# Rotary attention and a routed feed-forward on one core: logits of the last two head pairs in four tiles, the second group's gather placed behind them, and the order of the feed-forward's first blocks

## The chip, the cores and the metric

The kernel runs on one core of a Trainium2 chip. The metric is the device time in microseconds of one execution. Below, PE is the matrix engine (PEld its weight loads), DVE the vector engine, ACT the scalar engine, POOL the GpSimd engine and SP the sync engine, which here only starts DMAs.

## What is computed

```python
q_rot, k_rot = rotate(q), rotate(k)                 # 8 batches, 8 heads, 576 rows, 64 columns
scores = scale * q_rot @ k_rot.T
attn = exp(scores - max(scores)) ; attn /= sum(attn)
x = (attn @ v) as rows                              # 4608 rows of 512
h_dense = maximum(x @ w1_dense, 0) ; y_dense = h_dense @ w2_dense
expert_idx = argmax(x @ w_gate)                     # one of 8 experts for each row
gate_w = softmax(x @ w_gate)[expert_idx]
h = maximum(x[mask] @ w1[e], 0)                     # for each expert e, its rows
out = y_dense + gate_w * (h @ w2[e])
```

## The kernel before, in words

**Attention.** The loop of `attention` (L716) goes over 32 pairs of heads (`NP`), four to a batch, and one more turn for the last pair's output. Each turn `i` has nine steps `t`. In step `t` three things are put into the engines' queues by hand: the row maxima of pair `i + 2` (`s1_block`, while there is such a pair), one strip of logits of pair `i` (`s2_strip`: PE writes 128 x 512 into a tile of the tag `s2`, ACT takes the exponent into `pm`, L402), and a part of the product with the values for pair `i - 1` (`av_part`, L424). The tag `s2` has two buffers of one bank. Behind the nine steps come the tails of the strips (`s2_tails`, L409). `av_scale` divides by the sums on DVE, and `x_store` writes a batch's rows `xn` to the DRAM tensor `xd` (L451, L452, on SP's queue).

**PSUM.** The pool `attn_ps` has the tags `s1` (two buffers of two banks), `s2` (two of one bank) and `av` (one of two banks). From pair 29 on the value products use `s1`, and `av` is used by the sums of the routing (`attn_sums`) in turn 30.

**Routing.** Rows are sorted by expert into tiles of 128 rows, 4 tiles to a group. The first part (batches 0 to 5, 20 tiles, 5 groups) is planned while the last pairs of attention run. Its result `num` gives `take_i` (which rows a tile gathers), `put_i`, `gp` and `woff`. The second part (batches 6 and 7) is planned during the feed-forward, one piece of `plan` behind each of the first 12 tiles.

**Gather.** `gather` (L841) is an indirect DMA on POOL's queue that brings a tile's 128 rows from `xd` to `xg`; `turn` (L847) is a transposing DMA on SP's queue from `xg` to `xs`. `fetch` is both. `draw(g, u0)` (L853) does two tiles of group `g`, with their row numbers converted on DVE just before (`rows_of`, L829). In the kernel before, `draw` is put at turns and steps (30, 2), (30, 6), (31, 2), (31, 6) and twice at (31, 7): three groups, 12 tiles, all before the end of attention.

**Feed-forward.** `run_groups` (L940) goes over the groups and their tiles. For a tile, `expert_in` (L888) is one block of four 512-column matmuls on PE, then the gate and the rectifier on ACT into `hn` (L896); `expert_turn` transposes `hn` into `he` by a DMA on SP's queue (L901); `out_tile` (L904) is two blocks on PE (L908 with the dense half, L910 with the expert's), a copy on DVE (L912) and an indirect DMA that scatters the rows (L913, POOL's queue). The dense first half of a group is four blocks (`dense_in`, L884), each with a rectifier on ACT (L886). Each block needs all four tiles' `xs`, since it has the group's 512 columns. Before the loop the first group's four dense blocks stand at once; then each tile has its expert block, one dense block of the next group, and, once more than three tiles are open (`advance(3)`), an `out_tile`. Gathers of later groups go one or two to a tile (L965 to L974), ahead of the tile's expert block.

Of the kernel before, what the change touches and what calls it, by code (L numbers as in the profile page):

```python
# [13 lines left out]
bf16 = mybir.dt.bfloat16  # L14
# [7 lines left out]
P = 128  # L22
# [3 lines left out]
def kernel(  # L26
# [370 lines left out]
    def s2_strip(i, s):  # L397
        if s == 0:
            state["pm", i] = ap.tile([P, 9, S], fp16, tag="pm", bufs=2, name="pm")
        ps = pp.tile([P, 512], f32, tag="s2", bufs=2, name="s2")  # L400
        s2_mm(i, ps, s, False)
        nc.scalar.activation(state["pm", i][:, ORDER.index(s), 0:MAIN], ps, AF.Exp, scale=float(scale))  # L402

    def s2_tails(i, part):
# [154 lines left out]
    def plan_steps(k, wp, psum, st):  # L559
# [68 lines left out]
        def f():  # L628
            ts = slice(t0, t0 + NK)
            p5 = wp.tile([P, NPT, NK], f32, tag="p5", name="p5", **tl)  # L630
            nc.vector.tensor_copy(p5, ps["pt"])
            num = wp.tile([P, NK], f32, tag="num", name="num", **tl)
            nc.vector.tensor_tensor(num, p5[:, 0], p5[:, 1], AL.add)

            if k == 0:
                nums.append(num)
                rows_of(0, 2)
                rest = slice(3 * GT, NK)
                nc.vector.tensor_scalar(take_i[:, rest], num[:, rest], scalar1=-1.0, scalar2=0.0, op0=AL.add, op1=AL.max)
# [23 lines left out]
    def attention():  # L663
# [52 lines left out]
        for i in range(NP + 1):  # L716
            for t in range(9):
                if i + 2 < NP:
                    s1_block(i + 2, t)
                if i < NP:  # L720
                    s2_strip(i, t)
                if 1 <= i <= NP and t >= 1:
                    for k in range(*AVS[i % HP == 1][t]):
                        av_part(i - 1, k)
                    if t == 8:
                        av_scale(i - 1)
                if i == 0 and t in (3, 5):
# [12 lines left out]
                if t == 2 and i + LA < NP:  # L740
                    stage_transpose(i + LA)
                if t == 2:
                    for f, *x in loads.pop(i, ()):
                        f(*x)
                if (i, t) in WS:
                    n = WS.index((i, t))
                    load_w(*((w1d, moe_w1_dense), (w2d, moe_w2_dense))[n] if n < 2 else (w1e[:, n - 2], moe_w1[n - 2]))
                if t == 5:

                    if i % HP == 0 and i // HP + 1 < B:  # L750
                        stage_v(i // HP + 1)
                    if i % HP == 3 and HP < i < NP - HP or i == NP - 3:
                        x_store(i // HP - 1)
                    if i == NP - RA:
                        early_cm.__exit__(None, None, None)
                        open_late()
                        wa = late["wa"]
                        pl, mm, fin = plan_steps(0, wa, attn_sums, got0)
                        w2 = [lambda e=e: load_w(late["w2e"][:, e], moe_w2[e]) for e in range(E)]
                        steps[27, 6] = rk[0:1] + [route_parts]  # L760
                        steps[27, 5] = w2[0:2]
                        steps[27, 7] = w2[2:5]
                        steps[28, 0] = rk[1:2] + w2[5:6] + pl[0:1]
                        steps[28, 2] = gt[3:4]
                        steps[28, 3] = rk[2:3] + w2[6:8] + pl[1:2]
                        steps[28, 6] = rk[3:4]
                        steps[29, 0] = pl[2:3]
                        steps[30, 5] = pl[3:4]
                        steps[29, 3] = pl[4:6]
                        steps[29, 8] = rk[4:5]  # L770
                        steps[30, 0] = rk[5:6]
                        steps[30, 2] = mm + [fin, lambda: draw(0, 0)]
                        for n, at in enumerate(((30, 6), (31, 2), (31, 6))):
                            steps[at] = [lambda n=n: draw((n + 1) // 2, 2 * (n + 1) % GT)]
                        steps[31, 7] = [lambda: draw(2, 0), lambda: draw(2, 2)]
                if (i, t) == (NP - 2, 4):
                    logit_sum(B - 2)
                for st in steps.pop((i, t), ()):
                    st()
            if i < NP:  # L780
                s2_tails(i, 0)
            if i < NP:
                s2_tails(i, 1)
            if i in (0, 1) or i < NP and i % HP == 0:
                u0, u1 = (2 * i, 2 * i + 2) if i < 2 else (0, HP)
                for u in range(u0, u1, 2):
                    v_gate(u)
                v_part(i // HP, 0, u0, u1)
                steps.setdefault((i + 1, 0), []).append(lambda b=i // HP, u0=u0, u1=u1: v_part(b, 1, u0, u1))
        assert not steps and not v_steps and not loads  # L790
        logit_sum(B - 1)
        x_store(B - 1)
# [30 lines left out]
    got = []  # L823

    nums = []

    def rows_of(t0, n):
        ts = slice(t0, t0 + n)
        nc.vector.tensor_scalar(take_i[:, ts], nums[0][:, ts], scalar1=-1.0, scalar2=0.0, op0=AL.add, op1=AL.max)  # L829

    def room(g, pool, tag, bufs):
        m = sizes[g] if bufs == 1 else GT
        xg = pool.tile([P, m, DG], bf16, tag=f"xg{tag}", bufs=min(bufs, 2), name="xg")
        xs = pool.tile([P, m, DT, P], bf16, tag=f"xs{tag}", bufs=bufs, name="xs")
        got.append((xg, xs))

    def gather(g, u):
# [15 lines left out]
    def draw(g, u0):  # L853
        if u0 == 0:
            room(g, late["first"], g, 1)
        if (g, u0) != (0, 0):
            rows_of(g * GT + u0, 2)
        for u in range(u0, u0 + 2):
            fetch(g, u)

# [27 lines left out]
    def expert_in(t, xs, u):  # L888
# [3 lines left out]
        for dt in range(DT):  # L892
            nc.tensor.matmul(ps, lhsT=xs[:, u, dt, :], rhs=w[:, 0, dt, :], start=(dt == 0), stop=(dt == DT - 1))  # L893

        hn = fp.tile([P, F], bf16, tag="hn", bufs=3, name="hn")
        nc.scalar.activation(hn, ps, AF.Relu, scale=gp[:, t:t + 1])  # L896
        return hn, e

# [41 lines left out]
    def run_groups(gs, plan):  # L940
# [9 lines left out]
                w = todo.pop(0)  # L950
                out_tile(w["t"], w["hd"], w["u"], w["he"], w["e"])

        ahead = [(g, u) for g in gs if g >= len(got) for u in range(sizes[g])]
        known = len(plan)
        turns = []
        for st in dense_steps(gs[0]):
            st()
        for g in gs:
            n = sizes[g]
            dense = dense_steps(g + 1) if g + 1 in gs else []  # L960
            for u in range(n):
                t = sum(sizes[:g]) + u
                while turns:
                    turn(*turns.pop(0))
                for w in range(2):  # L965
                    if not ahead or ahead[0][0] > g + 3 or t < known and ahead[0][0] >= G1:
                        break
                    h, x = ahead[0]
                    if w and sum(sizes[:h]) + x > t + 12:
                        break  # L970
                    if x == 0:
# [56 lines left out]
```

## Time and profile before

| | us |
|---|---|
| median of 3 runs | 471.67 (471.66 to 476.84) |
| the profiled execution's own time | 471.43 |
| its span in the profile | 469.7 |
| PE busy | 405.4 |
| POOL busy | 342.4 |
| DVE busy | 320.4 |
| ACT busy | 295.0 |

The profiled execution's own time is 1.7 us over its span; what is read from the profile is set against this execution. The profile's views name a wait by what ended it: "issue" is time for which the profile shows no cause, "remote" and "another core or an unknown queue" are signals whose sender it could not name. Times in a timeline are counted from the span's start. Attention's last matmul ends near 328.4 us, and the feed-forward takes the rest.

### The profile page before, as it was taken

The numbers are of one execution on the slowest core, as the hardware profiler recorded it, in microseconds if no ns is written. First come the engines' busy times: TensorE is split into PE (matmuls) and PEld (weight loads), VectorE is DVE, ScalarE is ACT, GpSimd is POOL, SyncE is SP. The second block draws the span as 40 slices with busy tenths as digits, with TensorE's granted clock in tenths as the row PEclk, the third lists the DMA queues.
The fourth block names the chain that finished last, engine by engine and source line by source line (L and its number), as shares of the span: only waits on it lengthen the run. The fifth ranks groups of instructions, "written<-read, shape, count | busy, mean of one in ns | idle before, by whom it ended". The sixth has DMA issues, their size and how long they took to land.

```text
span 469.7 us, 11058 instructions
## 1 busy us (share of the span) xinstructions
PE 405.4 (86%) x4093; PEld 251.7 (54%) x4108; DVE 320.4 (68%) x583; ACT 295.0 (63%) x566; POOL 342.4 (73%) x279
## 2 busy tenths in 40 slices
PE   1788898899999998998998978736999998999992
PEld 1346566666666666666665656524444543444440
DVE  7886799899899999999998899911367311121221
ACT  6587887887887887897897767624633232333320
POOL 1899999989999799899999769571353465662332
PEclk9998999999999999999999989966999999999998
DMA  6866649987858867988969999673467469885352
GB/s 185 225 162 157 157 111 240 164 194 210 182 171 207 201 164 223 172 169 234 153 169 219 155 189 211 134 183 87 130 174 164 124 169 202 212 184 154 102 136 91
DMA packets 134251, 80.65 MB, mean 172 GB/s; under 512 B 93461, under 2 KB 127765, under 8 KB 134197
## 3 DMA queue, kind: packets, MB, share of 16 engines
q1 hardware_dynamic: 119684, 55.93, 50.6%
q0 software_dynamic: 14240, 23.73, 23.2%
q8 instruction: 35, 0.57, 0.5%
q10 hardware_dynamic: 272, 0.26, 0.2%
q14 instruction: 20, 0.16, 0.1%
HBM read 52.05 MB, written 14.42 MB: 142 GB/s over the span
## 4 chain that ended last, share of the span: by engine, by line
PE 64%; DVE 11%; ACT 9%; DMA 8%; issue 3%; another core or an unknown queue 2%; SPq 1%; POOLq 0%; POOL 0%; ACTq 0%; DVEq 0%
PE s L369 10%; PE av L424 9%; PE s L392 9%; PE py L910 7%; PE pd L884 7%; PE py L908 7%; PE pe L893 7%; DVE negm L371 5%; ACT pm L402 5%; DMA qT<-mT 3%; DMA kx<-qT 2%; PE vps L281 2%; PE s L365 2%; PE s L389 2%
## 5 line engine op out<-in xcount | busy, mean ns | idle before, releaser
L371 DVE TENSOR_REDUCE negm<-s 128x1 f32<-128x576 f32 x288 | 205.2, 750 | 20.1 <-PE s L369 18.5
L402 ACT ACTIVATE pm<-s 128x512 f16<-128x512 f32 x288 | 166.0, 598 | 54.7 <-PE s L392 39.3
L392 PE MATMUL s<-qT,kx 128*128 128x512 bf16 (+1 forms) x510 | 111.2, 290 | 13.0 <-ACT pm L402 8.2
L424 PEld LDWEIGHTS <-pm 128*128 128x128 f16 x1600 | 88.9, 99 | 60.1 <-issue 28.2
L369 PE MATMUL s<-kx,qT 126*128 126x288 bf16 x512 | 108.6, 295 | 6.0 <-DVE negm L371 4.2
L424 PE MATMUL av<-v,pm 128*128 128x82 f16 x1600 | 102.5, 203 | 1.0 <-DVE v L300 0.5
L314 POOL TENSOR_TENSOR ra<-qk,cosx 128x1152 bf16<-128x1152 f32 x30 | 78.9, 2629 | 19.4 <-DVE nat L317 10.7
L912 DVE COPY y<-py 128x512 f32<-128x512 f32 x37 | 25.2, 690 | 82.8 <-PE py L910 56.9
L913 POOL DMA_INDIRECT out_dram<-y,put_i x37 | 38.2, 1033 | 59.4 <-DVE y L912 42.7
L317 POOL TENSOR_TENSOR nat<-ra,rb 128x1152 bf16<-128x1152 bf16 x30 | 70.9, 2364 | 2.4
L896 ACT ACTIVATE hn<-pe,gp 128x512 bf16<-128x512 f32 x37 | 25.4, 687 | 66.1 <-PE pe L893 31.7
L841 POOL DMA_INDIRECT xg<-xd,take_i x37 | 35.9, 969 | 30.4 <-DMA xd<-xn 14.8
L369 PEld LDWEIGHTS <-qT 126*128 126x128 bf16 x512 | 40.5, 100 | 20.4 <-issue 12.3
L392 PEld LDWEIGHTS <-kx 128*128 128x128 bf16 x512 | 35.7, 97 | 12.2 <-issue 4.3
L315 POOL TENSOR_TENSOR rb<-qk,sinx 128x576 bf16<-128x576 f32 x30 | 42.1, 1405 | 0.0
L316 POOL TENSOR_TENSOR rb<-qk,sinx 128x576 bf16<-128x576 f32 x30 | 42.1, 1403 | 0.0
L893 PE MATMUL pe<-w1e,xs 128*128 x145 | 37.6, 379 | 1.8 <-ACT hn L896 0.8
L884 PE MATMUL pd<-xs,w1d 128*128 128x512 bf16 (+1 forms) x160 | 38.0, 363 | 0.4 <-ACT hd L886 0.3
L910 PE MATMUL py<-w2e,he 128*128 x145 | 37.5, 379 | 0.2
L908 PE MATMUL py<-w2d,hd 128*128 128x512 bf16 x141 | 37.1, 379 | 0.3
L886 ACT ACTIVATE hd<-pd 128x512 bf16<-128x512 f32 (+1 forms) x40 | 22.6, 564 | 15.1 <-PE pd L884 7.2
L389 PE MATMUL s<-qT,kx 128*64 128x512 bf16 x64 | 18.5, 289 | 14.5 <-issue 6.3
(173 smaller groups left out, 427.9 us busy)
## 6 DMA issues: line engine op xcount, KB each, us to landing
vf<-in_v_dram SPq DMA_DIRECT2D x8, 1024.0 KB
qk<-in_q_dram SPq DMA_DIRECT2D x15, 512.0 KB
qk<-in_k_dram SPq DMA_DIRECT2D x15, 512.0 KB
kx<-qT SPq DMA_DIRECT2D x30, 144.0 KB
xd<-xn SPq DMA_DIRECT2D x8, 512.0 KB
w1e<-in_moe_w_dram POOLq DMA_DIRECT2D x8, 512.0 KB
w2e<-in_moe_w_dram POOLq DMA_DIRECT2D x8, 512.0 KB
vf<-in_v_dram SPq DMA_DIRECT2D x16, 64.0 KB
```

Of the source, the lines that this page charges most:

```text
L314: eng.tensor_tensor(a, x, cx, AL.mult)
L315: eng.tensor_tensor(s[:, :, :, 0:half], x[:, :, :, half:D], sx[:, :, :, 0:half], AL.mult)
L317: eng.tensor_tensor(nat.rearrange("p c w d -> p w c d"), a, s, AL.add)
L369: nc.tensor.matmul(ps[:, c, 0:CH], lhsT=qT[:, t * P:(t + 1) * P], rhs=kT[:, k0 + c * CH:k0 + (c + 1) * CH], start=True, stop=True)
L371: nc.vector.tensor_reduce(state["negm", i][:, t:t + 1], ps[:, :, 0:CH], axis=AX.XY, op=AL.max, negate=True)
L392: nc.tensor.matmul(out_ap, lhsT=kT[:, s * P:(s + 1) * P], rhs=qT[:, qa if s < 4 else qb], start=True, stop=True)
L402: nc.scalar.activation(state["pm", i][:, ORDER.index(s), 0:MAIN], ps, AF.Exp, scale=float(scale))
L424: nc.tensor.matmul(state["av"][:, h, x * VC:(x + 1) * VC], lhsT=state["pm", i][:, 4 * h + n if n < 4 else 8, q0:q0 + P], rhs=v16s[b % VB][ ...
L884: nc.tensor.matmul(ps[:, 0:n], lhsT=w1d[:, dt, ft * P:(ft + 1) * P], rhs=xs[:, 0:n, dt, :], start=(dt == 0), stop=(dt == DT - 1))
L893: nc.tensor.matmul(ps, lhsT=xs[:, u, dt, :], rhs=w[:, 0, dt, :], start=(dt == 0), stop=(dt == DT - 1))
L908: nc.tensor.matmul(py, lhsT=hd[:, ft, u], rhs=w2d[:, ft, :], start=(ft == 0), stop=False)
L910: nc.tensor.matmul(py, lhsT=he[:, ft], rhs=w[:, 0, ft, :], start=False, stop=(ft == FT - 1))
```

## The change

- `s2_strip`: for the last two pairs (30 and 31) the strips 2 and 3, and 6 and 7, are computed two at a time into one two-bank tile of the tag `av`; the exponents are taken one strip at a time as before.
- The row numbers of groups 1 and 2 are put into a float tile `tk` by one DVE instruction when the plan is ready. `draw(1, 0)` and `draw(1, 2)` stand behind the whole of turn 31; an ACT copy that converts group 1's numbers into `take_i` stands ahead of them, in ACT's queue behind the last exponent. Nothing of group 2 is gathered in attention.
- Group 2 is gathered in the feed-forward, one tile behind each of the first four expert blocks, each with a small ACT copy for its row numbers. The rooms of groups 2 and 3 are made at the beginning. From the fifth tile on two tiles are gathered to a tile, until the first part's 20 are done.
- The feed-forward begins with the first tile's expert block. The first group's dense blocks come 0, 1, 1 and 2 behind its four tiles; those of groups 1 and 2 come two to a tile in group 1. In group 0 no `out_tile` is done (`advance(GT)`). A tile's gathers come behind its expert block, not ahead. `hn` has four buffers in place of three, and `room` makes `xs` before `xg`.

```diff
-        ps = pp.tile([P, 512], f32, tag="s2", bufs=2, name="s2")
-        s2_mm(i, ps, s, False)
+        if i < NP - 2 or s not in (2, 3, 6, 7):
+            ps = pp.tile([P, 512], f32, tag="s2", bufs=2, name="s2")
+            s2_mm(i, ps, s, False)
+        else:
+            if s % 2 == 0:
+                state["s2"] = pp.tile([P, 2, 512], f32, tag="av", bufs=1, name="s2w")
+                for x in range(2):
+                    s2_mm(i, state["s2"][:, x], s + x, False)
+            ps = state["s2"][:, s % 2]
...
+                nc.vector.tensor_scalar(tk, num[:, GT:3 * GT], scalar1=-1.0, scalar2=0.0, op0=AL.add, op1=AL.max)
...
-                        for n, at in enumerate(((30, 6), (31, 2), (31, 6))):
-                            steps[at] = [lambda n=n: draw((n + 1) // 2, 2 * (n + 1) % GT)]
-                        steps[31, 7] = [lambda: draw(2, 0), lambda: draw(2, 2)]
+                        steps[30, 6] = [lambda: draw(0, 2)]
...
+            if i == NP - 1:
+                draw(1, 0)
+                draw(1, 2)
...
+        xs = pool.tile([P, m, DT, P], bf16, tag=f"xs{tag}", bufs=bufs, name="xs")
         xg = pool.tile([P, m, DG], bf16, tag=f"xg{tag}", bufs=min(bufs, 2), name="xg")
-        xs = pool.tile([P, m, DT, P], bf16, tag=f"xs{tag}", bufs=bufs, name="xs")
...
-        if (g, u0) != (0, 0):
-            rows_of(g * GT + u0, 2)
+        if u0 == 0 and g:
+            nc.scalar.copy(take_i[:, g * GT:(g + 1) * GT], tk[:, (g - 1) * GT:g * GT])
+        if (g, u0) == (0, 2):
+            rows_of(u0, 2)
...
-        ahead = [(g, u) for g in gs if g >= len(got) for u in range(sizes[g])]
+        begin = gs[0] == 0
+        ahead = [(g, u) for g in gs if g >= 2 for u in range(sizes[g])] if begin else []
+        if begin:
+            room(2, late["first"], 2, 1)
+            room(3, fp, "", 4)
...
-        for st in dense_steps(gs[0]):
-            st()
+        dense = []
+        if not begin:
+            for st in dense_steps(gs[0]):
+                st()
         for g in gs:
             n = sizes[g]
-            dense = dense_steps(g + 1) if g + 1 in gs else []
+            for h in ((0,) if begin and g == 0 else (1, 2) if begin and g == 1 else (g + 1,)):
+                dense += dense_steps(h) if h in gs else []
             for u in range(n):
                 t = sum(sizes[:g]) + u
                 while turns:
                     turn(*turns.pop(0))
-                for w in range(2):
+                hn, e = expert_in(t, got[g][1], u)
+                todo.append({"t": t, "hd": hds[g], "u": u, "he": expert_turn(hn), "e": e})
+                for w in range(2 if t >= GT else 1):
...
-                    if w and sum(sizes[:h]) + x > t + 12:
+                    if w and sum(sizes[:h]) + x > t + 12 or t < GT and h > 2:
                         break
...
+                    if h == 2:
+                        nc.scalar.copy(take_i[:, 2 * GT + x:2 * GT + x + 1], tk[:, GT + x:GT + x + 1])
                     gather(h, x)
...
-                hn, e = expert_in(t, got[g][1], u)
-                todo.append({"t": t, "hd": hds[g], "u": u, "he": expert_turn(hn), "e": e})
-                for st in dense[FT * u // n:FT * (u + 1) // n]:
+                m = (0, 1, 1, 2)[u] if begin and g == 0 else -(-len(dense) // (n - u))
+                for st in dense[:m]:
                     st()
-                advance(3)
+                del dense[:m]
+                advance(GT if begin and g == 0 else 3)
```

More of the change, by code (lines that the diff above doesn't have):

```diff
@@ L825 @@
     nums = []
+    tk = route_p.tile([P, 2 * GT], f32)
     def rows_of(t0, n):
@@ L893, in expert_in @@
             nc.tensor.matmul(ps, lhsT=xs[:, u, dt, :], rhs=w[:, 0, dt, :], start=(dt == 0), stop=(dt == DT - 1))
-        hn = fp.tile([P, F], bf16, tag="hn", bufs=3, name="hn")
+        hn = fp.tile([P, F], bf16, tag="hn", bufs=4, name="hn")
         nc.scalar.activation(hn, ps, AF.Relu, scale=gp[:, t:t + 1])
@@ L968, in run_groups @@
                     h, x = ahead[0]
-                    if w and sum(sizes[:h]) + x > t + 12:
+                    if w and sum(sizes[:h]) + x > t + 12 or t < GT and h > 2:
                         break
-                    if x == 0:
+                    if h == len(got):
                         room(h, fp, "", 4)
+                    if h == 2:
+                        nc.scalar.copy(take_i[:, 2 * GT + x:2 * GT + x + 1], tk[:, GT + x:GT + x + 1])
                     gather(h, x)
                     turns.append(ahead.pop(0))
-                hn, e = expert_in(t, got[g][1], u)
-                todo.append({"t": t, "hd": hds[g], "u": u, "he": expert_turn(hn), "e": e})
-                for st in dense[FT * u // n:FT * (u + 1) // n]:
-                    st()
-                advance(3)
+                m = (0, 1, 1, 2)[u] if begin and g == 0 else -(-len(dense) // (n - u))
+                for st in dense[:m]:
+                    st()
+                del dense[:m]
+                advance(GT if begin and g == 0 else 3)
                 for st in plan.pop(0) if plan else ():
```

## The prediction, as put on record

> **What bounds the kernel now.** I read the page's header and chain first, then busy time by stretches, then the chain of waits and the timeline where the stretches look odd.
>
> ```profile
> span 469.7 us, 11058 instructions
> PEclk9998999999999999999999989966999999999998
> PE 64%; DVE 11%; ACT 9%; DMA 8%; issue 3%; another core or an unknown queue 2%; SPq 1%; POOLq 0%; POOL 0%; ACTq 0%; DVEq 0%
> ```
>
> PE carries the end, and one place stands out: the granted clock falls to 0.6 in two slices near two thirds of the span. Stretches around it (PE, PEld, DVE, ACT, POOL busy, then clock, DMA share, GB/s):
>
> ```profile
> 308.50:321.70 13.20, 4.05 (x30) 2.48 (x30) 0.00 (x0) 1.82 (x4) 7.65 (x9) 0.50 0.87 202
> 321.70:325.60 3.90, 3.25 (x28) 2.14 (x28) 0.00 (x0) 2.88 (x5) 0.00 (x0) 0.50 0.21 40
> 325.70:328.40 2.70, 2.53 (x65) 2.45 (x63) 1.28 (x3) 1.15 (x3) 0.00 (x0) 1.00 0.01 3
> 339.60:460.70 121.10, 119.23 (x589) 55.48 (x599) 39.16 (x81) 40.27 (x68) 57.54 (x57) 1.00 0.66 162
> ```
>
> For 13.2 us at the end of attention PE, DVE and ACT hardly work, while POOL and the DMAs are full. Behind 339.6 PE is 98% busy: there is nothing to gain there. The chain of waits across the odd place:
>
> ```profile
> 310.44 0.60 ACT pm L402
> 311.04 3.93 another core or an unknown queue
> 314.97 2.14 issue
> 317.11 0.60 ACT pm L402
> 317.71 3.97 another core or an unknown queue
> 321.71 0.61 ACT pm L402
> ```
>
> Attention's last products and the feed-forward's first blocks, from the same view:
>
> ```profile
> 326.49 1.95 PE av L424 x50
> 328.44 3.47 PE pd L884 x16
> 331.91 0.80 issue
> ```
>
> And PE's strips and ACT's exponents there, from the timeline:
>
> ```profile
> 310.36 0.59 PE L392 MATMUL s<-qT,kx 128*128 128x512 bf16 x1 [0.85 <-issue]
> 311.43 0.63 PE L392 MATMUL s<-qT,kx 128*128 128x512 bf16 x1
> 317.76 0.59 PE L389 MATMUL s<-qT,kx 128*64 128x512 bf16 x1 [5.36 <-issue]
> 302.38 2.73 ACT L402 ACTIVATE pm<-s 128x512 f16<-128x512 f32 x5 [2.36 <-PE s L392]
> 307.33 0.60 ACT L409 ACTIVATE pm<-s 128x512 f16<-128x512 f32 x1 [0.94 <-PE s L390]
> 309.71 1.33 ACT L402 ACTIVATE pm<-s 128x512 f16<-128x512 f32 x2 [1.19 <-PE av L424]
> 317.11 0.60 ACT L402 ACTIVATE pm<-s 128x512 f16<-128x512 f32 x1 [6.07 <-issue]
> 321.71 1.08 ACT L402 ACTIVATE pm<-s 128x512 f16<-128x512 f32 x2 [4.00 <-remote]
> 326.14 0.71 ACT L409 ACTIVATE pm<-s 128x512 f16<-128x512 f32 x2
> ```
>
> Pair 31's strip 2 is computed at 310.36 to 310.95, but its exponent starts at 317.11: PE's signal comes some 6 us late. Strip 3 ends at 312.06, its exponent starts at 321.71: nearly 10 us. The other way is prompt: the exponent ends at 317.71 and PE's next strip starts at 317.76. So the engines are free, and PE's signals to ACT are late. What runs meanwhile:
>
> ```profile
> 303.67 1.10 POOL L841 DMA_INDIRECT xg<-xd,take_i  x1 [4.88 <-ACT pm L402]
> 307.62 0.95 POOL L841 DMA_INDIRECT xg<-xd,take_i  x1 [0.30 <-issue]
> 308.87 0.94 POOL L841 DMA_INDIRECT xg<-xd,take_i  x1 [0.30 <-issue]
> 317.63 0.95 POOL L841 DMA_INDIRECT xg<-xd,take_i  x1 [0.30 <-issue]
> 306.64 15.74 SPq L847 DMA_TRANSPOSE xs<-xg  x12
> ```
>
> Twelve gathers go out 1.25 us apart (307.62 to 308.87) from 303.67 to 317.63, and their transposes, 1.31 us each (15.74/12), up to 322.4. Signals are prompt again at 321.7, 4.1 us behind the last gather's start, though transposes still land. I take the stall to be caused by gathers and transposes together.
>
> **The change part by part.** The sum is made against the profiled execution: 471.43 us, span 469.7, so 1.7 us around it, and 0.24 us under the median of 471.67.
>
> *Eight of twelve gathers leave attention.* Tiles 0 to 3 go out at the same places, 303.67 to 307.62. Group 1 waits for an ACT copy behind the last exponent, group 2 for the feed-forward. By the same 4.1 us signals are prompt at 307.62 + 4.1 = 311.7, not 321.7. From there the kernel before took 321.71 to 328.44 = 6.7 us to PE's end of attention, with strips 3 to 8 to exponentiate; now strip 2 is still open too, one more at 0.60, so 7.3 us. End: 311.7 + 7.3 = 319.0 against 328.44: **-9.4 us**. Bounds: were the signals late only as long as four transposes run (306.64 + 4 x 1.31, and some 3 us to land, as a gather takes from 303.67 to the first transpose at 306.64: 314.9), it is 322.2 and -6.2; were they never late enough to matter, pair 31 takes nine exponents and tails from 307.9, where pair 30's tails end (9 x 0.60 + 0.71 = 6.1) and the value products (1.95): 316.0, -12.4.
>
> *Two-bank tiles for strips 2, 3, 6, 7.* Same matmuls, same exponents. In turn 30 strip 3 now stands ahead of the routing sums in PE's queue, so its exponent falls into ACT's idle 2.36 us before 302.38: at most 0.6 us. With four tiles a late signal holds back fewer strips; only where signals are late. I count 0, as the -9.4 already ends the lateness; bound -0.6. The routing sums use the same tag's first bank; they come behind strip 2's exponent, which ends long before they start (DVE's one-hot holds them). Cost 0.
>
> *`tk` and ACT copies.* One DVE instruction more and four less. Five ACT copies, by the nearest rows 0.2 to 0.3 us each; the first stands behind the last exponent, where ACT is idle until its first rectifier. The four others stand behind `hn` of tiles 0 to 3:
>
> ```profile
> 337.18 0.86 PE pd L884 x4
> 337.22 0.69 ACT L896 ACTIVATE hn<-pe,gp 128x512 bf16<-128x512 f32 x1
> 339.14 0.60 ACT L886 ACTIVATE hd<-pd 128x512 bf16<-128x512 f32 x1 [1.24 <-PE pe L893]
> 336.85 0.26 ACT L488 ACTIVATE ex<-ex 128x80 f32<-128x80 f32 x1
> ```
>
> ACT then has 0.69 + 0.60 + 0.26 = 1.55 us for two PE blocks of 0.86 (1.73): covered, 0. Without cover it would be 4 x 0.26 = 1.0.
>
> *The feed-forward's order.* The number of blocks is the same, so PE's own time is too: 132.3 us from 328.44 to 460.7, the end of the last stretch above. Before, 0.80 us of "issue" stood ahead of the first expert block (331.91), and now it stands ahead of PE's first. New is that expert blocks 0 and 1 follow each other with no dense block between. Bounds 0 and another 0.80; I take **+0.4**. Held-back outputs (four of 1.73) come later in PE's order, at no cost while PE has other blocks, which it has.
>
> *Group 1's inputs.* The first tile's gather starts at 303.67, its transpose at 306.64: 2.97 us. Now the tails end 1.6 us before PE's end (326.85 to 328.44; call the end T), so gathers of group 1 start at T - 1.3, the last at T + 2.4, its transpose at T + 5.4, landing by T + 5.4 + 1.3 + some 1.5 = T + 8.2 (the landing is an estimate, half of the 2.97). PE needs all four at its first dense block of group 1, behind four expert blocks, four dense blocks and one expert block: T + 0.8 + 0.4 + 9 x 0.86 = T + 8.9. It just fits: 0. If it is late by 1 to 3 us, PE waits that long.
>
> *SP's and POOL's queues.* `x_store` of the last batch, and each `he`, now stand behind group 1's four transposes:
>
> ```profile
> 329.58 0.33 SPq L451 DMA_DIRECT2D xd<-xn  x1
> 333.40 0.94 POOL L841 DMA_INDIRECT xg<-xd,take_i  x1 [14.82 <-DMA xd<-xn]
> 337.16 0.95 POOL L841 DMA_INDIRECT xg<-xd,take_i  x1 [0.30 <-issue]
> 337.42 1.22 SPq L901 DMA_TRANSPOSE he<-hn  x1
> ```
>
> `he` 0 could go out near T + 2.4 (0.8 + 0.86 + 0.69) and goes near T + 7.4, `he` 1 2.5 us later, since a transpose of group 2 stands between. PE uses `he` 0 behind two dense blocks and half an output, T + 11.5. Covered, 0. The 14.82 us that POOL waited for `x_store` before cost nothing, and no gather now needs it so early.
>
> *Late signals in the feed-forward.* Eight gathers, 1.25 us apart, now start at T - 1.3. Expert block 2 needs `hn` 0 out of its PSUM buffer; between stand 1.73 us of PE work, of which ACT takes 0.69. A signal over 1.0 us late stops PE. Before, four gathers at the same spacing (333.40 to 337.16) beside transposes left signals prompt, but for one: the dense block that ended at 338.04 was read at 339.14, 1.1 us late. Later PE rides through far more:
>
> ```profile
> 395.38 0.69 ACT L896 ACTIVATE hn<-pe,gp 128x512 bf16<-128x512 f32 x1 [8.09 <-PE py L910]
> 394.42 2.34 PE py L910 x4
> ```
>
> ACT sat idle for 8 us there and PE lost about 1.5 (2.34 less 0.86). Bounds: 0, and the stall of before at its rate. That is (326.85 - 307.9 - 6.1)/12 = 1.07 us a gather, times 8 = 8.6. I take **+1.5**, near the feed-forward's own rows.
>
> A rule speaks against the change here: the Trainium skill, "TensorE: Matmul & The Clock Gate", Part 1, says the matrix engine falls to half clock after an idle window of about 3.4 us and comes back after a busy one. The trace agrees on the way back: PE resumed near 321.7 and has clock 1.00 from 325.7. By that rule one long stop in group 0 would add, as an estimate, half a window, 1.7 us, to my sum; no row of the feed-forward shows a clock under 1.00, so the sum leaves it out.
>
> Sum: -9.4 + 0.4 + 1.5 = -7.5. 471.4 - 7.5 = **463.9 us**.
>
> **The rivals.** *Full gain.* The four remaining gathers delay nothing that matters and the feed-forward rides through: -12.4, 459.0 us. For it: 333 to 341, four gathers and hardly a late signal. Against: with four gathers out ACT already stands idle for 0.94 us before 307.33 and 1.19 us before 309.71.
>
> *The stall moves.* Eight gathers delay the feed-forward's start at the old rate: -9.4 + 0.4 + 8.6 = -0.4, 471.0 us. For it: the same gathers and transposes, as dense as before, on engines with two PSUM buffers. Against: gathers of group 2 wait for ACT copies behind `hn`, so they slow down when signals do.
>
> *Slower: the lateness goes on through group 1.* From the fifth tile on two tiles are gathered to a tile where there was one, so 16 gathers fall on the first eight tiles. If each costs the 1.07 us of before, that is 17.1: 471.4 - 9.0 + 17.1 = 479.5 us. It is slower than before once a gather costs over 9.0/16 = 0.56 us. Against it: 333 to 341 again, and the 98% of PE behind 339.6, where gathers and scatters are dense too (POOL busy 57.5 us) and PE has other blocks to go on with.
>
> *The change does nothing to the stall*, because its cause is not the gathers: then 471.4 + 0.4, within the second rival.
>
> **How the numbers follow.** Mine 0.50, with its own range 460.5 to 467.5 (-12.4 + 1.5 and -6.2 + 0.8 + 1.5); full gain 0.25; the stall moves 0.17; slower 0.08 (the case that nothing is done to the stall is counted with the moved one). Some 2% is what a measurement of this kernel can tell from no change: 462.2 and 481.1 us. Faster by over 2%: most of the full gain (0.23) and a quarter of mine (0.12), 0.35. Slower by over 2%: half of the slower case, 0.04. Within: 0.61. The range 458.5 to 471.0 holds mine, most of the full gain and half of the moved stall, about 0.8.
>
> **What would show it.** Right: POOL shows four gathers from 303.7, then none until the last tails; pair 31's exponents run without idle over 1 us from 312; the last value products end near 319; the page's clock is under 0.9 in at most one slice there; PE's first feed-forward stretch of 12 us is over 85% busy. Wrong: idle of over 3 us before an exponent behind 312 (gathers are not the cause); PE idle of over 3 us before the fifth tile, with ACT waiting on "issue" or "remote" (the stall moved); PE's first dense block of group 1 waiting for `xs` (inputs late).

## The result and the profile after

| | before | after |
|---|---|---|
| median of 19 runs each, us | 474.70 (470.30 to 477.01) | 468.08 (465.26 to 471.55) |
| ratio | | 0.9868 [0.9844, 0.9893] |
| the profiled execution's own time, us | 471.43 | 465.76 |
| its span, us | 469.7 | 464.0 |

The change saves 1.3% (1.1 to 1.6%) on this chip; on another it saved 0.4% (below). The ratios here and below leave out executions over 1.5% above the fastest of their kernel, so they are not the quotients of the medians. The forecast was 463.9 us with a range of 458.5 to 471.0; the time lies inside, 4.2 us above the point. Of these 4.2, 3.0 come from the reference: 16 more runs of the kernel before moved its median from 471.67 to 474.70. Between the two profiled executions the step was forecast as -7.5 us and is -5.7. Behind that stand two errors of opposite sign: attention gave back more than forecast, and the feed-forward took more.

The header and chain of the profile after:

```profile
span 464.0 us, 11073 instructions
PEclk9999999999999999999999998989999999999998
PE 62%; DVE 11%; DMA 10%; ACT 9%; issue 3%; SPq 2%; another core or an unknown queue 1%; POOLq 0%; POOL 0%; ACTq 0%; DVEq 0%
```

The two clock slices at 0.6 of before are gone, but two at 0.8 stand there, and the chain has 10% DMA where it had 8%. The stretches around the place in the kernel after, with the columns as before (PE, PEld, DVE, ACT, POOL busy, clock, DMA share, GB/s):

```profile
308.50:312.00 3.50, 3.50 (x34) 2.20 (x33) 0.00 (x0) 2.66 (x5) 0.62 (x1) 0.64 0.85 187
312.00:317.00 5.00, 4.34 (x90) 3.81 (x89) 1.27 (x3) 2.85 (x7) 0.94 (x1) 0.91 0.40 30
317.00:322.50 5.50, 2.90 (x17) 1.16 (x14) 0.80 (x2) 0.72 (x3) 2.83 (x3) 1.00 0.58 143
322.50:329.00 6.50, 6.48 (x26) 2.68 (x26) 3.29 (x12) 4.32 (x12) 3.78 (x4) 0.74 0.83 221
336.00:455.00 119.00, 117.53 (x584) 54.06 (x583) 36.40 (x73) 39.34 (x66) 58.29 (x58) 1.00 0.73 167
```

PE now works right through the end of attention (308.5 to 317), the first 3.5 us still at a clock of 0.64. The hole has moved behind it, 317.0 to 322.5, and the half clock behind the hole, into the feed-forward. From 336 on PE is 99% busy, as before. The timeline of ACT and POOL there:

```profile
312.11 0.60 ACT L409 ACTIVATE pm<-s 128x512 f16<-128x512 f32 x1 [0.26 <-PE s L392]
313.35 1.08 ACT L409 ACTIVATE pm<-s2w 128x512 f16<-128x512 f32 x2 [0.65 <-PE s2w L392]
315.38 0.23 ACT L867 CAST take_i<-tk 128x4 int32<-128x4 f32 x1
321.78 0.69 ACT L908 ACTIVATE hn<-pe,gp 128x512 bf16<-128x512 f32 x1 [6.17 <-issue]
304.24 1.09 POOL L851 DMA_INDIRECT xg<-xd,take_i  x1 [4.88 <-ACT pm L409]
308.18 0.94 POOL L851 DMA_INDIRECT xg<-xd,take_i  x1 [0.30 <-issue]
315.88 0.94 POOL L851 DMA_INDIRECT xg<-xd,take_i  x1 [6.76 <-ACT take_i L867]
319.62 0.95 POOL L851 DMA_INDIRECT xg<-xd,take_i  x1 [0.30 <-issue]
```

The last exponents wait 0.26 and 0.65 us where they waited 6.07 and 4.00. Group 1's four gathers run from 315.88 to 319.62, and under them ACT stands idle for 6.17 us ahead of the first rectifier. What PE does in that time:

```profile
315.13 2.02 PE L431 MATMUL av<-v,pm 128*128 128x82 f16 x50
316.99 2.16 PE L905 MATMUL pe<-w1e,xs 128*128 x8
318.99 1.03 PE L896 MATMUL pd<-xs,w1d 128*128 128x512 bf16 x4
322.52 1.30 PE L905 MATMUL pe<-w1e,xs 128*128 x4 [2.50 <-ACT hn L908]
323.61 1.91 PE L896 MATMUL pd<-xs,w1d 128*128 128x512 bf16 x4
325.31 1.64 PE L905 MATMUL pe<-w1e,xs 128*128 x4
328.62 1.02 PE L905 MATMUL pe<-w1e,xs 128*128 x4
334.44 1.02 PE L922 MATMUL py<-w2e,he 128*128 x4 [0.48 <-DMA he<-hn]
335.91 1.03 PE L905 MATMUL pe<-w1e,xs 128*128 x4 [0.45 <-issue]
```

Attention ends at 315.13 + 2.02 = 317.15, against 328.44. The first two expert blocks (316.99, eight matmuls) follow without a gap. The first of them is four of the eight, so it ends near 318.0, but ACT starts on it only at 321.78: the signal is some 3.7 us late. Expert block 2 needs that buffer, and PE stops for 2.50 us. DVE is served as late. In the chain of waits:

```profile
315.43 6.21 another core or an unknown queue
...
321.67 0.23 DVE rz L442
...
327.99 6.31 DMA he<-hn
```

DVE's reciprocal of the last pair comes at 321.67, 4.5 us behind the products at 317.15. It starts 0.11 us ahead of ACT's rectifier, though the two wait for different matmuls. The same 0.11 us stands between them in two of the experiments below (327.17 and 327.28 in `e2_gathers`, 322.78 and 322.89 in `v3_banks`); in `e3_order` it is 0.74 us. That speaks for a hold on PE's side and against two readers that are each slow to start, but what is held the traces do not show. The last line is `he` 1, which takes 6.31 us to land. SP's queue shows why it starts so late:

```profile
307.22 16.61 SPq L857 DMA_TRANSPOSE xs<-xg  x8
323.92 0.53 SPq L458 DMA_DIRECT2D xd<-xn  x1
325.12 1.41 SPq L913 DMA_TRANSPOSE he<-hn  x1
326.62 1.27 SPq L857 DMA_TRANSPOSE xs<-xg  x1
327.99 1.24 SPq L913 DMA_TRANSPOSE he<-hn  x1
```

Group 1's transposes hold SP until 307.22 + 16.61 = 323.83; then come `x_store`, `he` 0, a transpose of group 2 and, at 327.99, `he` 1. It lands at 334.30, and PE has waited 0.48 us for it.

### The profile page after: what moved, and what is told of

Same layout as the page of the kernel before. It is cut to its first block, busy times and chain, and to the rows that moved or that the text cites. A ratio compares the mean times of both kernels' runs of the same rounds, so it can differ in the third digit from the quotient of the medians.

```text
span 464.0 us, 11073 instructions
## 1 busy us (share of the span) xinstructions
PE 404.8 (87%) x4108; PEld 250.0 (54%) x4108; DVE 320.5 (69%) x580; ACT 294.0 (63%) x571; POOL 342.3 (74%) x279
## 4 chain that ended last, share of the span: by engine, by line
PE 62%; DVE 11%; DMA 10%; ACT 9%; issue 3%; SPq 2%; another core or an unknown queue 1%; POOLq 0%; POOL 0%; ACTq 0%; DVEq 0%
PE s L369 10%; PE s L392 9%; PE av L431 9%; PE py L922 7%; PE py L920 7%; PE pe L905 6%; PE pd L896 6%; DVE negm L371 5%; ACT pm L409 5%; DMA qT<-mT 3%; DMA kx<-qT 2%; PE vps L281 2%; PE s L365 2%; PE s L389 2%; DMA vf<-in_v_dram 2%
## 5 line engine op out<-in xcount | busy, mean ns | idle before, releaser
L409 ACT ACTIVATE pm<-s 128x512 f16<-128x512 f32 x280 | 161.3, 598 | 42.0 <-PE s L392 36.1
L431 PEld LDWEIGHTS <-pm 128*128 128x128 f16 x1600 | 87.1, 98 | 53.8 <-issue 21.4
L392 PE MATMUL s<-qT,kx 128*128 128x64 bf16 (+1 forms) x504 | 107.0, 285 | 9.8 <-ACT pm L409 4.5
L431 PE MATMUL av<-v,pm 128*128 128x82 f16 x1600 | 100.5, 201 | 1.0 <-DVE v L300 0.7
L905 PE MATMUL pe<-w1e,xs 128*128 x148 | 38.9, 385 | 4.2 <-ACT hn L908 2.5
L443 DVE TENSOR_TENSOR xn<-av,rz 128x640 bf16<-128x640 f32 x32 | 26.4, 825 | 1.1
```

The source lines that it names most:

```text
L392: nc.tensor.matmul(out_ap, lhsT=kT[:, s * P:(s + 1) * P], rhs=qT[:, qa if s < 4 else qb], start=True, stop=True)
L431: nc.tensor.matmul(state["av"][:, h, x * VC:(x + 1) * VC], lhsT=state["pm", i][:, 4 * h + n if n < 4 else 8, q0:q0 + P], rhs=v16s[b % VB][ ...
```

## The experiments

The theory was that of the prediction: PE's signals come late while gathers and transposing DMAs run side by side, so fewer of both free attention. The rivals: the two-bank tiles do it, as a late signal then holds back fewer strips; the gathers alone do it; the transposes alone do it. For the feed-forward: the new order is a gain against a loss.

The kernel before has no single time: its median was 473.17 us on the chip of the first four kernels below, 469.37 (one run) on the next, 466.37 on a third and 474.79 on a fourth. Each kernel is compared with the kernel before on its own chip. Each run has one profiled execution; of the others only the time and the mean granted clock are known. "Attention's tail" is the time from the first gather's start to the last value product's end: 328.44 - 303.67 = 24.77 us before, 317.15 - 304.24 = 12.91 after.

**The two-bank tiles alone** (`e1_tiles`), on the kernel before:

```diff
-        ps = pp.tile([P, 512], f32, tag="s2", bufs=2, name="s2")
-        s2_mm(i, ps, s, False)
+        if i < NP - 2 or s not in (2, 3, 6, 7):
...
+            ps = state["s2"][:, s % 2]
```

> The kernel before with the two-bank tiles alone; all twelve gathers stay in attention. Theory (the traffic makes PE's signals late): PE still finishes attention behind 324 us, since exponents still wait for late signals while gathers run up to 318; the time falls by 0 to 3 us, ratio 0.993 to 1.0. Rival (too few logit buffers are the cause): PE finishes attention near 319, the feed-forward is as before, the time falls by 8 to 10 us, ratio 0.98.

Measured: 474.06 us, ratio 1.0016 [0.9986, 1.0045]. The tail is 24.4 us. ACT in its trace:

```profile
315.93 1.08 ACT L409 ACTIVATE pm<-s2w 128x512 f16<-128x512 f32 x2 [4.12 <-remote]
324.13 1.09 ACT L409 ACTIVATE pm<-s 128x512 f16<-128x512 f32 x2 [7.12 <-remote]
```

The waits of 4.12 and 7.12 us sum to 11.2; in the kernel before it was 1.19 + 6.07 + 4.00 = 11.3. More buffers alone change nothing that shows: the rival of the tiles falls.

**The change without the two-bank tiles** (`e2_gathers`), on the kernel after: the lines above undone.

> The changed kernel with the strips of the last two pairs in the old two single-bank tiles. Theory (traffic): four gathers instead of twelve already end the stall, PE finishes attention at 318 to 319.5, one or two us behind the changed kernel's 317.1, and the ratio to before is 0.987 to 0.992. Rival (buffers): the stall comes back, attention ends behind 324, ratio 1.0 or over, since the feed-forward's start stays longer.

Measured: 470.89 us, ratio 0.9942 [0.9904, 0.9980]. So moving gathers and order gains without the tiles. The expected 0.987 to 0.992 was a little too good. A variant that has the tiles, and other banks too (`v3_banks`, below), came to 0.9892 [0.9862, 0.9923] on the same chip: the tiles seem worth up to 0.5% once the gathers are moved, but the intervals touch. The profile shows a tail of 15.6 us, 2.7 more than with the tiles, where one or two more were expected; but that execution, 477.36 us, is far the longest of the four (the others 469.55 to 471.71), so what the tiles give is open.

**The change with the old order of the feed-forward** (`e3_order`), on the kernel after:

```diff
-        dense = []
-        if not begin:
-            for st in dense_steps(gs[0]):
-                st()
+        for st in dense_steps(gs[0]):
+            st()
...
-                advance(GT if begin and g == 0 else 3)
+                advance(3)
```

> The changed kernel with the feed-forward's old order: four dense blocks first, each later tile with one dense block of the next group, outputs from the fourth tile on. Theory (the order is there for group 1's late inputs): the first dense block of group 1 comes behind four dense blocks and one expert block, some 5 us behind PE's end of attention, and waits 3 to 5 us for its transposes, so the feed-forward takes 2 to 4 us more than the changed kernel's 137.8. Rival (late signals alone decide): no wait on transposes, the feed-forward within 1 us of 137.8.

Measured: 480.07 us, ratio 1.0105 [1.0037, 1.0174]: slower than before. Attention is as good as with the change (tail 11.8 us); the loss lies in the feed-forward, at two stops of PE, below with ACT's wait behind the first:

```profile
322.01 1.89 PE L896 MATMUL pd<-xs,w1d 128*128 128x512 bf16 x8 [3.48 <-ACT hd L898]
341.13 1.46 PE L896 MATMUL pd<-xs,w1d 128*128 128x512 bf16 x3 [6.67 <-DMA xs<-xg]
321.37 1.09 ACT L898 ACTIVATE hd<-pd 128x512 bf16<-128x512 f32 x2 [6.10 <-remote]
```

The first is the late signal, on `hd` instead of `hn`. The second is new: a dense block of group 2, whose gathers were put off furthest, waits 6.67 us for its transposes. Such a wait, of 3 to 5 us, was expected at group 1's first dense block; that one waits for nothing; the first stop has held PE back by then. The feed-forward takes 146.7 us, 9.0 more than with the change, where 2 to 4 were expected, and this execution (474.34 us) is the shortest of the four. So the moved gathers would lose all they gain if the order stayed; the order is no gain in itself but what makes room for later inputs.

**Expert blocks 2 and 3 in PSUM banks of their own** (`v3_banks`), on the kernel after, to take away PE's stop at 322.52:

```diff
-        ps = fpp.tile([P, F], f32, tag="pe", bufs=2, name="pe")
+        ps = fpp.tile([P, F], f32, **(dict(tag="py", bufs=3) if t in (2, 3) else dict(tag="pe", bufs=2)), name="pe")
```

> The changed kernel with the expert blocks of tiles 2 and 3 in banks of the outputs' tag, free at that time, so that PE can do six blocks of the feed-forward before it needs a signal back from ACT. Theory (the feed-forward's start loses by late signals on two buffers): PE's stop of 2.7 us ahead of the third expert block and the half clock of 3.4 us behind it vanish, span 460 us, 4 less than the changed kernel's 464.0, ratio to before 0.979. Rival (PE is then held by something else just behind, inputs or the dense blocks' buffers): the stop moves to the third dense block or the first of group 1 and the span falls by at most 1 us.

Measured: 468.05 us, ratio 0.9892 [0.9862, 0.9923]. The stop at 322.5 is gone, and others stand behind it:

```profile
324.24 1.02 PE L905 MATMUL pe<-w1e,xs 128*128 x4 [1.40 <-DVE lw L445]
327.27 1.02 PE L896 MATMUL pd<-xs,w1d 128*128 128x512 bf16 x4 [1.15 <-ACT hn L908]
335.35 1.02 PE L922 MATMUL py<-w2e,he 128*128 x4 [1.77 <-DMA he<-hn]
```

1.40 + 1.15 + 1.77 us take the place of 2.50 + 0.48 + 0.45. The span is 465.7 us and the feed-forward 138.2 (137.7 in the kernel after), so the theory, a span of 460, falls, and its rival holds. The banks were not free when the third expert block came: it waits for DVE's `lw`, which reads the last products. Room for PE to run ahead does not help while the next steps are late too: DVE with the last pair, the rectifiers and `he`.

**Which of the two, gathers or transposes.** First on the kernel before, all 12 gathers in attention but only group 0's four transposes there (`e4_gather_only`), the other eight behind the last `x_store`; and on the kernel after, its four gathers with eight more transposes, group 0's twice again (`e5_more_turns`; the extra transposes write the same data):

```diff
+        for g in (1, 2):
+            for u in range(GT):
+                turn(g, u)
...
-            fetch(g, u)
+            gather(g, u)
+            if g == 0:
+                turn(g, u)
```

```diff
-                        steps[30, 6] = [lambda: draw(0, 2)]
+                        steps[30, 6] = [lambda: draw(0, 2)] + [lambda u=u: turn(0, u) for u in range(GT)] * 2
```

> The kernel before, with all twelve gathers in attention but only the four transposes of group 0; the eight of groups 1 and 2 stand behind the last store of attention. Theory (gathers and transposes together make PE's signals late): exponents of pair 31 wait no more than some 2 us in all behind 312, PE ends attention at 317 to 320. Rival (gathers alone do it): the exponents still wait up to about 321, PE ends attention near 328. In both the feed-forward's start pays for the late transposes, some 10 us of inputs, which is no verdict.

> The changed kernel with group 0's four transposes done three times, so that twelve transposes run in attention beside four gathers. Theory (both together): behind the fourth gather, from 312 on, the exponents run as in the changed kernel and PE ends attention at 317 to 318.5; the eight transposes more cost only DMA time. Rival (transposes alone make signals late): exponents wait until some 322, PE ends attention at 325 to 328.

Measured, one run each beside 469.37 of the kernel before: 466.21 and 470.87 us. In neither is there a stall in attention: tails of 10.2 and 10.3 us, no idle between pair 31's exponents. Taken alone this says that neither does it without the other. But the kernel before was not profiled on this chip. Its one execution there has a mean granted clock of 0.960, as low as the profiled ones with the stall (0.963 to 0.970), against 0.982 for `e4_gather_only`; that hints at a stall but is no proof, since `e5_more_turns`, which has none in attention, has 0.967. So both were run again on one chip together with the kernel before, unchanged (`before_again`).

> The kernel before unchanged, for its profile on the chip of the next two. Theory (gathers beside transposes make PE's signals late): exponents of pair 31 stand idle some 11 us in all and attention ends 24 to 25 us behind the first gather, as in the first profile. Rival (the stall is a property of a chip or of an execution, not of the kernel): on some chips the exponents idle under 2 us and attention ends 11 to 13 us behind the first gather; then the kernel's time is some 6 us shorter too.

> Twelve gathers and four transposes in attention, as before, beside a profile of the kernel before on the same chip. Theory (both together): where the kernel before shows the stall, this one ends attention 10 to 13 us behind the first gather. Rival (gathers alone): 20 us or more behind it.

> Four gathers and twelve transposes in attention, as before, beside a profile of the kernel before on the same chip. Theory (both together): where the kernel before shows the stall, attention ends 10 to 14 us behind the first gather. Rival (transposes alone): 20 us or more behind it. In both the feed-forward's start is late, since group 1's transposes stand behind eight that were not needed.

Measured, beside 474.79: before again 474.86, ratio 1.0031 [0.9994, 1.0067]; gathers without transposes 479.45, 1.0136 [1.0078, 1.0194]; transposes without gathers 472.39, 0.9958 [0.9923, 0.9993]. The same stretch of each, in this order before, gathers, transposes; the fourth row is the first run of the gathers, on the other chip:

```profile
308.50:320.00 11.50, 3.39 (x24) 2.02 (x24) 0.83 (x6) 1.91 (x4) 8.53 (x10) 0.55 0.86 192
```

```profile
308.50:320.00 11.50, 4.17 (x33) 2.48 (x32) 1.53 (x7) 2.61 (x5) 8.76 (x10) 0.67 0.60 150
```

```profile
308.50:320.00 11.50, 7.72 (x119) 5.97 (x117) 1.28 (x3) 5.62 (x12) 3.75 (x5) 0.83 0.72 141
```

```profile
308.50:320.00 11.50, 8.40 (x128) 6.12 (x128) 5.54 (x18) 6.17 (x14) 8.76 (x10) 1.00 0.94 189
```

PE is busy for 3.39, 4.17, 7.72 and 8.40 us of 11.5. Tails: 24.7, 25.0, 13.0 and 10.2 us. ACT in the second kernel, its last gather and its transposes:

```profile
318.06 0.60 ACT L402 ACTIVATE pm<-s 128x512 f16<-128x512 f32 x1 [4.43 <-remote]
323.08 1.09 ACT L402 ACTIVATE pm<-s 128x512 f16<-128x512 f32 x2 [4.42 <-remote]
319.55 0.95 POOL L844 DMA_INDIRECT xg<-xd,take_i  x1 [0.31 <-issue]
308.54 5.23 SPq L850 DMA_TRANSPOSE xs<-xg  x4
```

On this chip, where the kernel before stalls, twelve gathers stall as long with four transposes as with twelve. The four have gone out by 308.54 + 5.23 = 313.77, and the exponents wait on until 318.06 and 323.08, 9.3 us later, while only gathers go out, the last at 319.55. Four gathers beside a full queue of transposes have the tail of the kernel after, 13.0 us. (SP issues 16 transposes there in 21.61 us from 306.82, 1.35 each, so seven or eight of the twelve start before attention ends at 316.94.) So the theory as I had it falls here: the transposes are not needed, the run of gathers is what counts. The load of the DMA engines does not order the cases either: 0.60 at 150 GB/s with the stall, 0.94 at 189 GB/s without. And the last row is the same program as the second: the same gathers, POOL busy for the same 8.76 us, and no stall. So the run of gathers is not sufficient: the two executions, on two chips, differ in something that the traces do not show. If the kernel before did stall on that other chip, as its clock hints, the transposes counted there; that stays open. The slower ends of these two kernels are their own: the eight transposes put off cost a wait of their own (first row, gathers), the eight extra ones keep PE from group 0's inputs (second row, transposes):

```profile
340.08 1.46 PE L889 MATMUL pd<-xs,w1d 128*128 128x512 bf16 x3 [4.14 <-DMA xs<-xg]
```

```profile
321.63 0.59 PE L905 MATMUL pe<-w1e,xs 128*128 x1 [4.69 <-DMA xg<-xd,take_i]
```

**A version that might beat both.** Two versions, run on the third chip, kept all 12 gathers in attention and put only the transposes off: group 1's behind the last `x_store`, group 2's one to a tile (`v5_early_gathers`); the second has the PSUM banks of `v3_banks` as well (`v6_early_banks`). The kernel after ran beside them (`after_again`).

```diff
-                        steps[30, 6] = [lambda: draw(0, 2)]
...
+                        steps[31, 2] = [lambda: draw(1, 0), lambda: draw(1, 2)]
+                        steps[31, 7] = [lambda: draw(2, 0), lambda: draw(2, 2)]
...
-            fetch(g, u)
+            gather(g, u)
+            if g == 0:
+                turn(g, u)
```

> The changed kernel with all twelve gathers in attention again, but the transposes of group 1 behind the last store of attention and those of group 2 one to a tile in the feed-forward. Theory (only gathers and transposes together make PE's signals late): pair 31's exponents run as with gathers alone, PE ends attention some 10 to 11 us behind the first gather; at the feed-forward's start no gather runs beside the transposes, so hn of tile 0 is prompt, the stop of 2.7 us and the half clock are gone and the feed-forward takes 133 to 135 us in place of 137.7; ratio to before 0.972 to 0.98. Rival (transposes with he alone suffice for late signals at the start, or group 1's transposes come too late): feed-forward 137 us or more, ratio 0.985 or over.

> The same with the expert blocks of tiles 2 and 3 in the outputs' banks as well. Theory: with prompt signals the buffers no longer matter, within 0.002 of the kernel without them. Rival: signals are still late, and the banks gain 2 us.

> The changed kernel unchanged, for a comparison on this chip: ratio to before 0.985 to 0.990.

Measured, beside 466.37: 463.59, ratio 0.9957 [0.9931, 0.9984]; 463.49, 0.9943 [0.9913, 0.9973]; the kernel after 465.13, 0.9964 [0.9934, 0.9994]. The three intervals overlap, so no version is shown to be better than the change. On this chip the change gains 0.4% (0.1 to 0.7%), not 1.3%. The expected 0.972 to 0.98 and 0.985 to 0.990 were too good. All three have tails of 10.3 or 10.4 us: signals to attention were prompt here, twelve gathers or four. They were prompt at the feed-forward's start too. The first rectifier and the first dense block of group 1 in the kernel after, on this chip:

```profile
316.47 0.69 ACT L908 ACTIVATE hn<-pe,gp 128x512 bf16<-128x512 f32 x1 [2.49 <-issue]
327.35 3.25 PE L896 MATMUL pd<-xs,w1d 128*128 128x512 bf16 x8 [3.66 <-DMA xs<-xg]
```

Attention ends at 315.52 and the first expert block near 316.3, so the rectifier at 316.47 is not late, though eight gathers follow each other 1.25 us apart from 314.25 to 323.01. PE does not stop before 323.7; then it waits 3.66 us for group 1's inputs. The feed-forward takes 138.8 us here, 136.2 and 135.7 in the two versions, where 133 to 135 was expected of the first. The kernel before was not profiled on this chip. That it stalls less here is only argued, from its 466.37 us and its mean granted clock: 0.968 to 0.989 in 29 executions, against 0.947 to 0.974 in 29 on the fourth chip. On a chip like the fourth I would expect the versions with 12 early gathers to lose what `e4_again` lost; that was not run.

## Why the prediction was right and where it was wrong

- **"I take the stall to be caused by gathers and transposes together."** Half right. Gathers are the cause that can be switched where the stall shows: with eight taken out the tail is 12.9 us for 24.8. Transposes beside four gathers leave it at 13.0. The two always ran together in the one trace I had, so it could not tell them apart. (Nor was POOL full in that stretch, as the prediction has it: it is busy for 7.65 of 13.2 us.)
- **Eight gathers leave attention, -9.4.** Right mechanism, wrong size: 328.44 to 317.15 is -11.3, and -11.9 from the first gather on. The step that failed is "By the same 4.1 us signals are prompt at 307.62 + 4.1 = 311.7". The last early gather started at 308.18, so prompt signals were due at 312.3. Exponents were prompt from 308.81 on: pair 31 lost 1.3 us between its exponents, where the rule allows for 312.3 - 308.8 = 3.5. A constant read off one stall of twelve gathers was carried to a run of four; in fact the lateness was small in this run of four. With a tail of 10.3 us for the same program on the third chip, four gathers held attention by some 2.6 us and twelve by 14.5. The full gain of -12.4, given 0.25 as a rival, was nearer for this stage, but it was no bound: it counts from 307.9, where pair 30's exponents were late already. Their tails end 4.9 us behind the first gather before the change, and 2.6 in `e4_gather_only`.
- **Two-bank tiles 0.** Right alone (1.0016). With the gathers moved they may be worth up to 0.5%; the bound of -0.6 us was too tight then, if the touching intervals mean anything.
- **The feed-forward's order +0.4.** In the trace, -0.8: the gap of 0.80 us ahead of the first expert block did not move to the front, it is gone (316.99 follows the products at once). I had taken it for a cost of whichever block comes first; what it was in the old order stays open (that block has records of three of its four matmuls, so some 0.2 us of the gap may be the fourth), but it is no such cost.
- **Late signals in the feed-forward, +1.5.** The step that failed: "near the feed-forward's own rows". Under group 1's four gathers in a row, 315.88 to 319.62, PE's signals were 3.7 us late to ACT and 4.5 us to DVE, not 1.1 (on the third chip they were not late at all). The cost is the stop of 2.50, the small waits of 0.48 and 0.45, and the half clock (next point): 2.50 + 0.93 + 1.8 = 5.2, less the 0.80 gone, 4.4. The feed-forward's length went from 132.2 to 137.7 us, +5.5; the rest of some 1 us is not explained (PE's waits behind 340 sum to 1.2 us, before to 1.1).
- **Group 1's inputs, 0.** No wait in this execution, but by luck: PE came to group 1's first dense block at 329.48, T + 12.3 and not T + 8.9, since the stop and the half clock had held it. On the third chip nothing held it and the block waited 3.66 us. The step that failed there is the landing of "some 1.5": the last of group 1's transposes left SP's queue at 322.40, T + 6.9, and PE went on at 327.35, T + 11.8, so the inputs took some 5 us to land.
- **SP's and POOL's queues, 0.** The places in the queue came as worked out: `he` 0 near T + 7.4 = 324.6 (measured 325.12), `he` 1 2.5 us later at 327.1 (327.99). What the step left out is the landing, 6.31 us for `he` 1; it was covered but for 0.48 us, and only because PE had already lost its 2.50.
- **The clock.** PE's granted clock is 0.50 from 323.10 to 326.50:

```profile
319.70:323.10 3.40, 0.90 (x5) 0.32 (x4) 1.36 (x4) 1.32 (x4) 1.15 (x2) 1.00 0.84 188
323.10:326.50 3.40, 3.40 (x10) 1.22 (x8) 2.52 (x9) 2.07 (x7) 2.22 (x3) 0.50 0.74 229
```

  A block of four takes 1.30, 1.91 and 1.64 us there and 1.02 behind it (rows 322.52 to 328.62 above): 0.28 + 0.89 + 0.62 = 1.8 us lost. The rule of the Trainium skill that spoke against the change, "TensorE: Matmul & The Clock Gate", Part 1, gave 1.7 as an estimate, by half a window, and the sum left it out because no row of the feed-forward of before showed a low clock. That was the wrong test: the rows of before had no stop there, and the change made one. The Trainium skill speaks there of an idle window of about 3.4 us; here a stretch of 3.40 us in which PE worked for 0.90 was enough. A stop need not cost it: behind the one of 3.48 us in `e3_order` eight matmuls take 1.89 us, and the granted clock from 322.0 to 324.0 is 1.00.
- **The range and the signs to look for.** Right: four gathers from 304, none until the last tails; no exponent waits over 1 us from 312; no wait for group 1's inputs. Wrong: two slices of the clock under 0.9, not one (attention still has one, 0.64 from 308.5 to 312); PE's first 12 us of the feed-forward 2.90 + 6.48 = 9.4 us, 78%, not 85%. The stall did move, at about a third of its old size (4.4 of 12.9 us): the second rival had the place right, and my own case the size of the sum. The total came out near only because -11.3 and +5.5 miss -9.4 and +1.9 by 1.9 and 3.6 us on opposite sides; that was luck. The 2% taken for what a measurement can tell was too coarse: the interval here is 0.5% wide.

## What to carry to other kernels

When all engines stand idle and the readers of one engine's results start long behind its ends, look at what runs in the background, and count the length of its run (here indirect gathers 1.25 us apart): where the stall showed, attention's tail was 24.4 to 25.0 us with twelve in a row and 11.8 to 13.0 with four and the change's tiles, against 10.2 to 10.4 where nothing was late. Put such runs where PE has other work and free buffers; moved to the start of a stage with two buffers, they made signals late again on the chips where twelve had stalled attention. Whether gathers set further apart would hold signals less was not run. A stop that a change makes can bring its own clock penalty, whether or not the old trace shows one, so give the half clock a chance in the sum: it cost 1.8 us behind the stop of 2.50, and nothing behind the one of 3.48. And compare on more than one chip: the same change gave 1.3% and 0.4%.

## What the hardware showed that was not expected

- PE's signals to ACT and DVE can come late by 3.7 and 4.5 us while four gathers run and by nearly 10 while twelve do, while ACT's to PE are prompt.
- The same program stalls in its profile on one chip (tail 25.0 us, DMA share 0.60) and not in that on another (10.2 us, 0.94). The kernel before differs by 8 us between chips (466.37 and 474.79). Why is open: the traces show late signals but not what holds them, and no run here separates the chips' causes. That four gathers delay the feed-forward's first signals by 4 us in the profiled execution, yet delayed attention's by less at 304 to 308, is open too. The chips go together in both places. Where twelve gathers stall attention, the first signals of the feed-forward are late as well (DVE's reciprocal 4.5 us behind the products in the kernel after, 4.55 in `v3_banks`, 4.9 in `e5_again`). On the two chips without a stall in attention they are prompt (0.04 us in `e5_more_turns` and in `after_again`).
